# Ranking on TensorE by a triangle matrix, shared angles, and denominators by accumulating DMAs in a fused routing-attention and gated-convolution kernel

## The chip, the cores and the metric

The kernel runs on one core of one Trainium2 chip. The metric is the device time of one execution in microseconds (us). TensorE is called PE here (PEld are its weight loads), VectorE DVE, ScalarE ACT, GpSimd POOL, SyncE SP. A queue name such as SPq is the instruction stream in which an engine issues DMAs.

## The reference

Two parts in a row, all in f32, with batch B = 4, 8 heads, sequence S = 768, head size 64, 16 clusters.

```python
q_assign = argmax(q_n @ c_n, axis=-1)          # nearest of 16 centroids, per head
k_assign = argmax(k_n @ c_n, axis=-1)
mask = q_assign[..., :, None] == k_assign[..., None, :]
scores = where(mask, q @ k.T / 8, -1e9)
attn = exp(scores - max); attn = attn / (sum(attn) + 1e-9)
x = (attn @ v) as [B, S, 512]
x1, x2, x3 = split(x @ w_proj, 3)
x2_conv = irfft(rfft(x2, axis=seq) * rfft(filter, axis=seq))
out = (x1 * x2_conv * x3) @ w_out
```

`argmax` takes the first of equal largest values. Inputs are q, k, v (4, 8, 768, 64), centroids (8, 16, 64), w_proj (512, 1536), filter (768, 512), w_out (512, 512); the output is (4, 768, 512).

## The kernel before

The program is a plan: `build` makes a list of some 1,900 operations, each with the engines that may do it, and `ORDER`, a string written out in the source, gives the order in which they are emitted, the engine of each and the PSUM banks of each matmul group. A word such as `P275:31` is operation 275 on PE, into banks 3 and 1; the letters are P (PE), A (ACT), V (DVE), G (POOL), S (SP). Within one engine the order of the words is the order of its queue. The costs and due times in the source were used to make the string; at run time only the string and the data dependences count.

**Routing and attention.** The 32 heads are taken as 8 groups `n` of four heads, each in two pairs `pr`. `routing(n)` transposes q and k of a group on PE, copies them to `qkP`, casts them to bf16 into `aug`, and makes the masks: products with the normed centroids (`sim`, L582) on PE, two transposes to tokens on DVE (L587), the largest value (L595), equality with it (L596), then for the first of equal values a product with falling weights (L598), another maximum (L601), a difference (L602), the transpose back (L605), and a clip of the k half (L607). DMAs (`masks`, L482) put the 16 rows into `aug`, so that the score matmul adds 0 where the clusters agree and a large negative number elsewhere. Group 0 has its own form of this (`first_masks`).

`attention(n, pr)` has six steps over blocks of 128 keys. A step is three score groups on PE (`sc`), three exponentials of 128x512 on ACT (`exp`, L646 and L649), and eight matmuls with v in f32 (`pv`, L660). The exponentials are also summed over the blocks into `acc` on DVE (L681), the first two blocks by three smaller additions on DVE or POOL (L677). The sum over the 128 partitions gives the softmax denominators. It is done in two ways, chosen by `FIRST`: for groups below `FIRST` and for the last group by matmuls with ones (`den`, L694); for the others by three accumulating DMAs issued by POOL (64, 32 and 16 rows added, L714), a way through memory (L718, L720), a reduce on DVE (L724) and an added constant (L725). Both go on with a reciprocal (L727), a way through memory (`dr`, `rb`) and the division that writes `xT` (L760).

**Convolution.** `hyena(b)` follows each two groups: token products (`U`, L797), spectra (`spectrum`), products with the filter's spectrum (L821, L825), the inverse (`I`), gates (`G`), and the output products (`W`), copied to `ob` and stored. It fills PE between the steps of later groups. For the last batch row block 5 is copied as a whole and stored by one DMA (L919, L922).

**Start.** `angles` makes the sine tables `fw` from index products reduced to one turn, all on DVE, from half-integer indices `s0t` which `half` (L964 to L967) makes on DVE; `tables` transposes them and transforms the filter.

Of the kernel before, what the change touches and what calls it, by code (L numbers as in the profile page):

```python
# [34 lines left out]
FIRST = 2  # L35
# [89 lines left out]
V0 G30 A35 S45 A46 P14:0 G18 S47 P2:1 A48 P9:2 G27 V22 S49 P6:3 P10:4 G24 S52 P1:5 V59 P4:6 G23 V36 V37 S51 P12:7 V38  # L125
V60 A39 G25 P13:0 V53 A50 G17 V61 P8:1 A40 G20 V54 P16:2 V62 G34 P11:3 V55 P5:4 G19 P15:5 P3:6 V21 V56 A63 P68:7 V41
P70:0 A66 G29 A58 P76:1 S121 A64 P74:2 A57 P7:3 V26 G65 P42:4 G32 S123 V71 A67 P146:5 V69 G28 P138:6 S124 P140:3 V44
P149:0 V43 G152 P142:7 A77 V141 S122 P94:4 V75 A147 P96:3 A148 V95 A79 P144:1 P102:2 S126 V72 P100:5 A145 V78 P80:4
S125 A101 V103 A97 P82:1 S127 V81 A98 G105 P108:5 S128 V83 A151 G73 A139 P106:3 A104 V84 S120 V85 G132 P251:2 A99 S242
V86 S134 V107 A150 P245:4 G133 V87 P249:1 S135 A246 P243:6 V88 A252 S130 G33 V89 A250 G31 A244 S131 P257:0 G137 V90  # L130
A248 P255:3 V91 S286 V92 P183:2 V93 A258 V109 P185:1 S129 G247 A256 P187:6 V143 P190:0 A184 V110 S288 P261:4 G136 V111
P263:5 A262 P192:3 V112 P194:7 A264 V113 P200:2 G358 A186 P267:45 V114 A191 V115 A188 G197 A193 P202:1 V268 P204:0
P208:6 A203 V269 P210:3 G198 A195 P212:1 V270 P189:45 A201 A211 V199 A205 P216:7 V117 P196 V271 A116 A209 V119 V207
P218:2 A217 P220:3 P224:0 A213 P226:6 P206 A118 V153 A225 V155 P228:7 A221 P293:1 P214 V157 A219 V272 A229 V160 A227
P295:0 P222 A294 V154 A296 V158 P297:3 V215 P230 A298 A259 P300:2 V273 P302:7 A232 G156 P304:6 P310:1 P312:0 A303
P299:45 A301 V274 A305 V161 P314:3 A311 P306 V162 A254 V275 G159 A266 P318:7 P320:2 P322:6 S280 A313 V223 P164:1 A315
S278 P163:0 A165 S292 P316 A167 V276 A319 V231 S277 P172:3 A321 P178:7 S283 A323 P171:2 S279 A169 P326:6 V166 G308
P324 S287 A327 V168 A175 S285 V170 G309 P328:0 A173 P233:6 S284 V176 A329 S290 P330:1 V174 G253 A234 P177:0 A331
P334:3 S291 V179 P336:6 G307 A181 P338:2 P359:1 V180 S235 P332 A339 V182 S282 A337 G260 A265 S281 P361:0 P419:267 V317
A335 A362 A360 P363:3 P340 S454 V421 A420 A422 V325 S236 A364 P366:0 S289 P368:1 A342 P370:2 P376:6 S453 P378:7 A371  # L140
V333 P380:3 P365:45 A367 S418 A381 A369 P384:2 V237 P386:0 V341 A377 P388:3 S238 P392:1 A385 P372 A387 A379 V373
P394:6 A389 P343:2 V375 V374 P427:073 A344 V383 A393 S239 A395 S240 P396:2 P400:1 A430 S352 P402:6 P382 A401 V391 S345
A403 S458 A428 P390 A397 S456 A429 V399 A424 P404:1 P461:6 P435:20 A431 V241 A405 S346 A423 P463:3 G434 V437 S455
P465:7 P468:1 A462 V436 P398 A466 G353 S457 G354 V407 A464 A469 P470:6 P472:0 P478:2 A425 P406 V438 G426 A473 G356
V439 P480:7 P482:3 A408 P486:1 P409:0 V440 A471 V441 A487 P467:45 G476 A410 V347 A479 S348 A481 G355 V475 P488:6 S411
P490:1 P494:0 A489 V442 P496:2 P498:7 A483 P502:6 V443 G477 P474 A499 A495 S446 A497 V444 P484 V485 A491 S445 A503
S448 P504:3 P701:702 S412 V493 S447 S460 P506:1 P492 A507 S452 V501 A702 S350 A703 P500 S349 A505 S520 V509 P639:6
S459 P641:1 P643:3 A640 P508 A642 V413 A704 G432 S414 A644 P646:6 P648:1 S449 G357 V433 P511:0 A649 A510 V654 P650:2
P656:7 P658:3 A512 V351 P660:1 A647 P645:45 S513 A657 G653 S735 A659 P664:0 A651 S450 P666:6 P668:7 A661 P672:3 V655
S451 P652 A667 S415 V663 A673 S514 A669 P674:2 P709:163 S416 A665 A675 S737 V671 P676:7 S736 P662 A712 A677 V710 A711  # L150
P680:0 V515 P682:2 V679 S516 P684:7 P743:1 A683 P745:3 P670 A685 A681 V417 A713 P717:62 V687 A744 S517 A708 S518
P747:7 P750:0 P752:1 V719 G689 P678 A751 V718 A746 G706 V720 A714 P686 A748 V721 P754:0 P760:2 V722 A688 P762:6 P764:3
V723 P768:7 A753 P749:45 A763 V519 A755 P770:1 A761 V758 P772:6 P521:0 A769 G690 V724 A765 P776:2 V759 A771 P778:7
P523:3 A779 V725 G705 A522 P531:1 A777 S734 V524 P533:7 A773 V726 V757 S733 P780:0 P784:2 G691 V525 P756 A781 S727
V767 S728 S730 P766 S729 V775 S742 P526:6 S738 P786:3 P528:0 A527 V707 S740 A785 V783 P774 A532 S739 S700 P788:6
P805:2 V534 S732 G715 P807:1 A789 P782 V529 A787 S692 A806 S741 V530 G537 P809:6 P812:3 V535 P814:2 P790 A813 V536
A815 V539 A808 P867:073 V791 A810 A792 S693 P816:2 P540:1 A870 V538 S731 G793 P543:6 A869 P811:45 V541 S804 A817 A868
V544 V542 P822:2 G546 P548:0 A823 V545 P824:3 P826:7 P830:1 P556:2 V547 A831 P551:6 V549 A874 G820 P818 V552 A827 V550
A825 G554 P559:1 P832:7 V553 P834:3 P564:0 A833 V555 G794 A835 P838:6 P566:7 V557 A565 G819 P568:3 V558 V567 P840:0
P828 A569 G821 V694 A872 V560 A841 P875:273 G716 V561 A839 V695 A871 G795 V829 S696 P842:0 S903 P846:1 A876 P836 A878  # L160
S904 V563 A877 A847 V837 P848:6 P883:23 A849 S698 A843 A881 G562 S796 P850:7 V884 P909:1 P911:6 S907 V885 P844 A912
V845 S697 A851 A910 S901 P572:02 P913:3 S797 P916:6 A573 V886 G873 P918:7 P920:1 A917 S866 P852 V574 A919 S902 V887
A914 P926:6 P928:7 V575 P570:3 A927 V888 A854 P930:0 V853 P579:2 A921 P581:6 A931 P915:45 A580 V699 A879 A882 V889
P583:1 G576 A929 P934:0 V571 P585:2 G890 A584 V798 A935 P587:73 V586 P936:1 V799 P938:0 P922 A937 S800 V577 G855 A939
V891 A588 G925 P942:2 P932 V590 S894 V589 S896 V892 V578 P944:1 S893 P594:0 S801 V923 P596:3 S895 V582 P946:7 P940
V924 S906 A947 A945 V933 S905 A943 G856 P950:6 P952:7 A595 P954:1 S802 P598:2 A951 S908 V597 A880 P948 V941 S898 A953
S970 A955 P1089:0 P1091:6 P1093:3 A1090 P1096:7 P1098:1 V949 A1092 P1100:0 P956 A1094 A1101 A599 G857 P1106:6 V957
A1097 P600:3 A1099 P1151:027 A1107 A958 V592 G959 P1108:1 P1110:6 A1152 V1153 P1095:45 A1109 V601 A1154 V803 A1111
P1114:1 P1116:3 V591 P1159:027 S858 A1117 G593 S900 A1115 S897 P602:63 A1160 V1161 S1191 P1118:1 V1162 P1102 A603
A1119 S899 G960 V605 S859 V604 P1167:02 V1103 S1185 V1105 S1192 G607 P1122:7 V1169 S1187 P1124:1 P609:3 V1168 A1125  # L170
G606 S1188 P1126:6 A1156 V1170 P1130:0 P1132:2 P611:1 S1189 G961 A1131 V1171 A1123 P1112 S1186 A1158 V1172 V608 A610
P1134:0 P1193:7 A1127 P1120 V1173 A1165 G1104 A1135 V860 P613:3 V1113 P615:6 A614 S962 A1163 P1195:0 P1197:3 P1128
A1196 V861 G1155 V612 S862 A1133 V616 A1194 P1200:0 P1202:1 V1121 A1198 P1136 A1201 A1203 P1204:2 V1174 S963 P617:67
A1138 S863 V1129 P1210:3 A1205 P1212:0 P1214:1 S864 A618 P1199:45 A1213 S1190 A1211 V1208 A1215 P1218:2 S1150 P1220:0
V1207 P1222:3 P1226:1 A1221 P1206 V1137 A1223 A1219 P1228:0 P1230:3 V1175 P1234:2 G1209 P1216 A1231 A1235 V964 A1229
G1139 V965 P1236:3 V619 P1238:2 S966 P1224 A1237 V620 A1157 V622 V621 A1239 P1317:036 V865 A1227 V1217 P1325:721 S967
A1320 S968 A1166 S1254 P1232 A1164 V623 A1319 G1140 V1225 A1326 P1240 A1318 A1327 P624:0 V1176 A1242 V969 S1179 P626:3
A625 S1180 V1233 A1328 S1177 P981:6 S1178 P971:0 A982 S1182 G1141 V1241 P973:1 A972 A627 P629:2 V974 G1243 P983:7 V975
P976:6 V984 V1322 P978:0 S1142 A977 V985 S1358 P1255:3 P1257:1 V979 P1259:6 A1256 P631:7 S628 A1260 V980 G986 A1258
P1262:3 P1264:6 P1266:0 P1272:1 A1265 V987 P1261:45 S1143 G1244 A1273 V989 S1355 A1263 V988 A630 P990:6 S1353 P993:1  # L180
A632 V991 P1014:3 S1316 A1267 V992 P1016:2 S1181 G1271 A1015 V994 S1183 P998:7 V995 P1274:0 S633 P1276:6 P1280:3 A1275
V996 P1018:1 S1351 G997 V999 P1001:0 A1019 P1268 A1281 V1002 A1277 V1000 G1004 P1282:1 V1003 P1006:3 A1283 P1284:6
# [46 lines left out]
def build(T):  # L229
# [385 lines left out]
    def attention(n, pr, sins):  # L615
# [88 lines left out]
        if not last:  # L704
# [5 lines left out]
            else:  # L710
# [12 lines left out]
                def gather(e):  # L723
                    T.nc.vector.tensor_reduce(T.dn, T.dp[:].rearrange("p r b -> p b r"), axis=AX, op=Alu.add)  # L724
                    T.nc.vector.tensor_scalar(T.dn, T.dn, EPS * S, None, op0=Alu.add)  # L725
# [467 lines left out]
```

## Time and profile before

| | |
|---|---|
| median of 3 runs | 368.99 us (368.93 to 369.77) |
| the profiled execution | 369.5 us, span of the trace 367.7 us |
| PE, DVE, ACT, POOL busy | 354.2, 345.0, 269.3, 131.9 us |
| mean granted PE clock | 0.994 |
| DMA moved | 45.69 MB, mean 124 GB/s |

The span runs from the first to the last instruction of the trace. Busy time is the union of an engine's instructions; the share of busy time is an average over stages with different limits, so the stages are looked at one by one. In the strips of the page the span has 40 slices, 9.2 us each, and a digit is a busy share in tenths.

### The profile page before, as it was taken

The page shows a single profiled execution, that of the slowest core. Times are in us where ns is not written, and L with a number is a line of the kernel's source. Part 1 is how long each engine was busy: PE and PEld are TensorE (multiplying, and loading weights), DVE is VectorE, ACT ScalarE, POOL GpSimd, SP SyncE. Part 2 cuts the span into 40 slices and gives each one's busy share as a digit, 9 for nine tenths or more (in the row PEclk, how much of TensorE's full clock was granted, in tenths as well). Part 3 has the DMA queues.
Part 4 walks back from the last instruction along what each step waited for, and adds up shares of the span by engine and source line. Part 5 has one row for each costly group of instructions (what it writes and reads, how often), then busy time and mean ns, then how long its engine had stood idle before and what let it go on. Part 6 is the DMA issues. An engine that isn't in the chain of part 4 may idle for free.

```text
span 367.7 us, 8518 instructions
## 1 busy us (share of the span) xinstructions
PE 354.2 (96%) x3269; PEld 211.6 (58%) x3269; DVE 345.0 (94%) x476; ACT 269.3 (73%) x501; POOL 131.9 (36%) x162
## 2 busy tenths in 40 slices
PE   7879999999999999999999999999989999999994
PEld 3535555455455556655565666665646666567782
DVE  8999999996999999988999999999989999999993
ACT  5979999979785789596986777989858665533251
POOL 7770250533032552425231542413330543135600
PEclk9989999999999999999999999999999999999999
DMA  9994156579555767599775957666553554110124
GB/s 171 235 252 94 29 119 184 101 124 214 122 74 121 161 104 146 99 178 154 101 180 104 210 142 174 111 116 109 92 78 70 146 102 112 47 44 2 59 116 172
DMA packets 88004, 45.69 MB, mean 124 GB/s; under 512 B 76488, under 2 KB 82012, under 8 KB 87964
## 3 DMA queue, kind: packets, MB, share of 16 engines
q1 hardware_dynamic: 82508, 34.77, 40.9%
q0 software_dynamic: 2960, 9.77, 17.7%
q10 hardware_dynamic: 2496, 0.62, 0.9%
q8 instruction: 25, 0.41, 0.5%
q14 instruction: 15, 0.12, 0.1%
HBM read 31.59 MB, written 7.40 MB: 106 GB/s over the span
## 4 chain that ended last, share of the span: by engine, by line
PE 60%; DVE 22%; DMA 6%; issue 5%; ACT 3%; SPq 1%; POOL 1%; DVEq 0%; POOLq 0%; ACTq 0%
PE bank L69 30%; PE pair L660 19%; DVE acc L681 7%; PE bank L797 3%; DMA rb<-dr 3%; DMA aug<-ohT 2%; PE bank L582 2%; PE bank L551 2%; PE bank L67 2%; ACT tm L442 1%; ACT p L649 1%; DVE tm L809 1%; DMA dr<-dn 1%; DVE acc L677 1%; DVE hm L446 1%
## 5 line engine op out<-in xcount | busy, mean ns | idle before, releaser
L660 PE MATMUL pair<-p,vraw 128*64 128x385 f32 x768 | 140.4, 488 | 0.0
L649 ACT ACTIVATE p<-bank 128x512 f32<-128x512 f32 x192 | 109.0, 607 | 22.9 <-PE bank L69 18.5
L681 DVE TENSOR_TENSOR acc<-p,acc 128x1536 f32<-128x1536 f32 x64 | 113.0, 1766 | 2.9 <-POOL acc L677 1.2
L660 PEld LDWEIGHTS pair<-p,vraw 128*64 128x64 f32 x768 | 56.4, 136 | 47.4 <-issue 40.1
L69 PE MATMUL bank<-aug,aug 80*64 80x256 bf16 (+3 forms) x706 | 79.2, 326 | 2.6 <-DMA aug<-ohT 1.5
L646 ACT ACTIVATE p<-bank 128x512 f32<-128x512 f32 x96 | 57.4, 607 | 14.6 <-PE bank L69 13.6
L69 PEld LDWEIGHTS <-aug 80*64 80x64 bf16 (+1 forms) x706 | 43.4, 109 | 41.0 <-issue 28.9
L69 PE MATMUL bank<-xT,wpj 128*64 128x384 bf16 x504 | 50.0, 326 | 0.0
L714 POOL DMA_DIRECT2D acc<-acc x30 | 23.9, 796 | 58.8 <-DMA acc<-acc 29.1
L69 PEld LDWEIGHTS <-wpj 128*64 128x64 bf16 x504 | 33.4, 110 | 11.0 <-issue 3.7
L677 POOL TENSOR_TENSOR acc<-p,p 128x512 f32<-128x512 f32 x21 | 27.0, 1297 | 32.2 <-DVE acc L677 11.5
L246 ACT CAST aug<-qkP 64x768 bf16<-64x768 f32 x43 | 35.4, 829 | 0.7
L69 PEld LDWEIGHTS <-y 128*64 128x64 bf16 x496 | 28.2, 110 | 10.2 <-issue 3.0
L246 ACT COPY qkP<-bank 128x512 f32<-128x512 f32 (+1 forms) x50 | 25.7, 551 | 9.4 <-PE bank L69 7.0
L248 POOL CAST aug<-qkP 64x768 bf16<-64x768 f32 x16 | 14.1, 884 | 42.5 <-DVE xT L760 17.9
L821 DVE TENSOR_TENSOR tm<-bank,hm 128x512 f32<-128x512 f32 x44 | 27.9, 683 | 0.8 <-POOL y L825 0.2
L69 PE MATMUL bank<-wout,y 128*64 128x512 bf16 x192 | 24.5, 379 | 0.1
L825 POOL TENSOR_TENSOR y<-tm 128x512 bf16<-128x512 f32 x14 | 17.8, 1276 | 14.6 <-DVE tm L821 10.0
L797 PE MATMUL bank<-wpj,xT 128*64 128x512 bf16 x192 | 22.8, 380 | 0.0
L899 POOL TENSOR_TENSOR y<-yy,x 128x768 bf16<-128x768 f32 x6 | 11.0, 1825 | 26.9 <-DVE yy L896 19.4
L677 DVE TENSOR_TENSOR acc<-p,p 128x512 f32<-128x512 f32 x27 | 18.3, 701 | 0.4 <-ACT p L646 0.3
L246 ACT COPY ob<-bank 128x512 f32<-128x512 f32 x20 | 11.4, 592 | 9.8 <-PE bank L69 9.8
(163 smaller groups left out, 457.6 us busy)
## 6 DMA issues: line engine op xcount, KB each, us to landing
vraw<-in_v_dram SPq DMA_DIRECT2D x16, 384.0 KB, 5.7
qkraw<-in_k_dram SPq DMA_DIRECT2D x31, 192.0 KB, 4.9
qkraw<-in_q_dram SPq DMA_DIRECT2D x30, 192.0 KB, 4.2
rb<-dr SPq DMA_DIRECT2D x30, 192.0 KB, 3.7
out_dram<-ob SPq DMA_DIRECT2D x11, 512.0 KB, 4.7
acc<-acc POOLq DMA_DIRECT2D x10, 384.0 KB, 5.0
acc<-acc POOLq DMA_DIRECT2D x10, 192.0 KB, 4.2
wpj<-in_moe_w_proj_dram POOLq DMA_DIRECT2D x4, 384.0 KB, 6.2
```

Source lines behind the costliest of these rows:

```text
L69: T.nc.tensor.matmul(out[64 * i:64 * i + 64], lhsT[:, 64 * i:64 * i + 64], rhs, start=start, stop=stop)
L246: T.nc.scalar.copy(out, in_)
L248: (T.nc.vector if e == "DVE" else T.nc.gpsimd).tensor_copy(out, in_)
L646: T.nc.scalar.activation(o, ap(h).rearrange("p (a b) -> p a b", a=2), Act.Exp, scale=0.125)
L649: T.nc.scalar.activation(flat(s)[:, lo:lo + 512], ap(h), Act.Exp, scale=0.125)
L660: T.nc.tensor.matmul(o[64 * hp:64 * hp + 64, ch, :385], T.vraw[vs][:, hp, sk * D:(sk + 1) * D], T.p[slots[sk]][:, hp, 384 * ch:384 * ch + ...
L677: alu(e).tensor_tensor(o, x, y, op=Alu.add)
L681: T.nc.vector.tensor_tensor(T.acc[os], T.p[slots[sk]][:, :, :S], T.acc[os], op=Alu.add)
L714: op(("POOL", .8), lambda e, rows=rows: T.nc.gpsimd.dma_start(flat_()[:rows], flat_()[rows:2 * rows], accum_op=Alu.add), te, r=[], w=AK, b ...
L797: T.nc.tensor.matmul(ap(h)[64 * i:64 * i + 64], T.xT[xs][:, kt, tokens(m, i, w_)], T.wpj[:, kt, DM:2 * DM], start=kt == 0, stop=kt == ND - 1)
L821: op(("DVE", .68), lambda e, i=i, cs=cs, r=r, h=h: T.nc.vector.tensor_tensor(T.tm[r][:, cs], ap(h), hmrow(i, (0, 2, 2, 3)[2 * r + cs]), op ...
L825: op({"POOL": 1.3, "DVE": .68}, lambda e, i=i, r=r: alu(e).tensor_tensor(T.y[:, i, r], T.tm[r][:, 0], T.tm[r][:, 1], op=Alu.add if r else ...
```

## The change

Four edits, and a new `ORDER` for all operations with 1,963 words instead of 1,936.

1. Groups 1 to 7: L598, L601, L602 and L607 are gone. The equality words are transposed, multiplied on PE by a 128x128 matrix `tri` (blocks of 16: 1 on the diagonal, -2 for earlier clusters; the k half times 262144) into two banks, and four clips of 64x384 on ACT or DVE bring them back to `ohT`. POOL makes `tri` at the start. The masks wait for the clips of both chunks.
2. The angles: POOL makes odd integers directly, `half` is gone, `s1t` is one POOL instruction; some angle instructions may be on ACT (Copy, Abs) or POOL, and for the second table one DVE instruction becomes a product (DVE) and a sum (POOL).
3. `FIRST` from 2 to 1: the two pairs of group 1 get their denominators by accumulating DMAs. In that way the constant is added on ACT instead of DVE (L725).
4. The last output row is copied in halves on ACT and DVE, and stored by two DMAs, issued on ACT and SP.

```diff
-FIRST = 2
+FIRST = 1
...
-                op(("POOL", 1.1), lambda e, w_=w_, m=m: T.nc.gpsimd.indirect_dma_start(
+                op(("POOL", 1.7), lambda e, w_=w_, m=m: T.nc.gpsimd.indirect_dma_start(
...
-        op({"DVE": .58, "POOL": 1.8}, lambda e: alu(e).tensor_tensor(
-            words(), words(), T.revx[:].unsqueeze(1).to_broadcast([128, 48, NC]), op=Alu.mult), b0 + 4, r=["revx"],
-           w=both("oh"), lock=True)
-        op(("DVE", .95), lambda e: V().tensor_reduce(m2(), words(), axis=AX, op=Alu.max), b0 + 4.1, r=both("oh"), w=both("m2"))
-        op({"DVE": .75, "POOL": 1.8}, lambda e: alu(e).tensor_tensor(words(), words(), bc(m2()), op=Alu.subtract),
-           b0 + 4.2, r=both("m2"), w=both("oh"), lock=True)
...
-        op(("DVE", .38), lambda e: V().tensor_scalar(T.ohT[64:], T.ohT[64:], -1.0, 1.0, op0=Alu.max, op1=Alu.add), due,
-           r=both("ohT"), w=both("ohk"), lock=True)
+        h2 = Bank(cls, 2)
+
+        def rank(e, h=h2):
+            for ch in range(2):
+                columns(bank(h.ids[ch])[:, :384], T.tri[:], T.ohT[:, ts(ch, 384)], True, True)
+        op(("PE", .325), rank, due, r=both("ohT") + both("ohk") + ["tri"], w=[h2], alloc=h2, kind="proj")
+        for ch in range(2):
+            for j in (1, 0):
+                def clip(e, ch=ch, j=j, h=h2):
+                    o, x = T.ohT[64 * j:64 * j + 64, ts(ch, 384)], bank(h.ids[ch])[64 * j:64 * j + 64, :384]
+                    if e == "DVE":
+                        V().tensor_scalar(o, x, 0.0 if j else -1.0, None, op0=Alu.max if j else Alu.add)
+                    elif j:
+                        T.nc.scalar.activation(o, x, Act.Relu)
+                    else:
+                        T.nc.scalar.activation(o, x, Act.Copy, bias=-1.0)
+                op({"ACT": .48, "DVE": .55}, clip, due + .6 + .1 * ch, r=[h2], w=[("ohk" if j else "ohT", ch)], free=[h2])
...
-                    T.nc.vector.tensor_scalar(T.dn, T.dn, EPS * S, None, op0=Alu.add)
-                op(("DVE", .68), gather, te + 6, r=["dp"], w=["dn"], kind="port")
+                op(("DVE", .48), gather, te + 6, r=["dp"], w=["dn"], kind="port")
+                op(("ACT", .22), lambda e: T.nc.scalar.activation(T.dn, T.dn, Act.Copy, bias=EPS * S), te + 6.1, r=[], w=["dn"])
...
+                if last and tt == 2 and e_:
+                    for c, e in ((0, "ACT"), (1, "DVE")):
+                        op((e, .37), lambda e, c=c, ob=ob, h=h: copy(e, ob()[:, 1, ts(c, 256)], ap(h)[:, ts(c, 256)]), due + 1,
+                           r=[h], w=[(obk[1], c)], free=[h], after=[])
+                        op({"SP": .6, "ACT": .6}, lambda e, c=c, ob=ob: dma(e)(
+                            T.out[b].rearrange("(p t) m -> p t m", t=NT)[:, 5, ts(c, 256)], ob()[:, 1, ts(c, 256)]), due + 2,
+                           r=[(obk[1], c)], byts=131e3)
+                    continue
...
-        def half(e):
-            for i in range(2):
-                h = T.s0t[64 * i:64 * i + 64]
-                T.nc.vector.tensor_scalar(h[:, :2 - i], h[:, :2 - i], 0.5 - 383.0 * i, None, op0=Alu.add)
-            h = T.s0t[64:, 1:]
-            T.nc.vector.tensor_scalar(h, h, -1.0, 767.5, op0=Alu.mult, op1=Alu.add)
-            T.nc.vector.tensor_scalar(T.s1t, T.s0t, 1.0 / S, None, op0=Alu.mult)
-        op(("DVE", 1.0), half, .3, r=["s0t0"], w=["s0t", "s1t"])
+        op({"DVE": .3, "POOL": .3}, lambda e: alu(e).tensor_scalar(T.s1t, T.s0t, 0.5 / S, None, op0=Alu.mult), .3,
+           r=["s0t"], w=["s1t"])
...
+        def tri(e):
+            G().memset(T.tri, 0.0)
+            sel = lambda op_, fill, pattern: G().affine_select(out=T.tri, in_=T.tri, compare_op=op_, fill=fill, base=0,
+                                                               pattern=pattern, channel_multiplier=1)
+            sel(Alu.is_ge, -2.0, [[-1, 128]])
+            sel(Alu.not_equal, 1.0, [[-1, 128]])
+            sel(Alu.is_ge, 0.0, [[-16, 8], [0, 16]])
+            G().tensor_scalar(T.tri[:, 64:], T.tri[:, 64:], BIG, None, op0=Alu.mult)
+        op(("POOL", 1.5), tri, 10, w=["tri"])
```

In the new `ORDER` the operations that the prediction names stand as follows ("..." for words left out). Group 2's transposition is V446 and its ranking P447, P481 is a `pv`; groups 3, 5 and 7 have V733 and P734, V1189 and P1190, V1645 and P1646. G518 is the first accumulating DMA of group 1's second pair, P531 the first `U`. At the end P1958 finishes the last row's matmuls, V1961 and A1959 copy its halves, and A1951 and S1952 are the copy and the store of rows 2 and 3.

```diff
... V446 P481 A504 G413 V484 A498 P447:13 A502 V350 G431 P505:7 S351 P509:0 A448 V450 P511:2 A449 P491 ...
... V1189 P1234 A1183 G1226 A1247 P1254:6 A1253 P1190:72 P1242 ...
... P1953:1 P1958 P1954 P1940 V1961 P1942:5 V1955 S1962 A1941 P1943 S1956 P1947
P1949:3 A1944 V1948 P1950 S1945 A1951 A1959 S1952 A1960
```

The costs of some operations in the source are also set anew (for example the indirect DMA above); they have no effect at run time.

More of the change, by code (lines that the diff above doesn't have):

```diff
@@ L130 @@
[L130 to L134, printed above, removed]
@@ L150 @@
[L150 to L154, printed above, removed]
```

260 lines of the change are left out of this document (145 added, 115 removed).

## The prediction

> **What bounds the kernel now.** I read the page first, then the busy time by stage, the chain, the waits, the groups kept apart by shape, and the start and the end instruction by instruction. Part 1 of the page and the strips of part 2:
>
> ```profile
> span 367.7 us, 8518 instructions
> ...
> PE 354.2 (96%) x3269; PEld 211.6 (58%) x3269; DVE 345.0 (94%) x476; ACT 269.3 (73%) x501; POOL 131.9 (36%) x162
> ...
> PE   7879999999999999999999999999989999999994
> ...
> DVE  8999999996999999988999999999989999999993
> ...
> PEclk9989999999999999999999999999999999999999
> ```
>
> Two engines are nearly full, so the question is which one sets the end. The table by stage (columns: stretch, its length, busy time and count of PE, PEld, DVE, ACT, POOL, then clock, DMA share, GB/s) answers it:
>
> ```profile
> 0.00:9.00 9.00, 6.53 (x29) 3.26 (x29) 7.43 (x25) 4.99 (x10) 6.81 (x30) 1.00 0.94 170
> 9.00:20.00 11.00, 8.11 (x79) 4.77 (x79) 10.55 (x24) 10.78 (x23) 8.25 (x23) 1.00 1.17 244
> 20.00:35.00 15.00, 14.59 (x105) 7.71 (x107) 14.27 (x25) 12.49 (x25) 5.71 (x6) 0.89 0.83 178
> ...
> 50.00:75.00 25.00, 25.00 (x209) 12.87 (x208) 24.37 (x25) 24.18 (x46) 8.01 (x9) 1.00 0.60 137
> ...
> 355.00:368.00 13.00, 8.03 (x83) 5.42 (x79) 6.49 (x10) 2.73 (x6) 0.00 (x0) 0.95 0.33 129
> ```
>
> PE is idle for 367.7 - 354.2 = 13.5 us in all: 2.47 + 2.89 + 0.41 = 5.8 before 35 us, 12.7 - 8.03 = 4.7 after 355, and so only 3.0 in the 320 us between. DVE work taken out there can win back at most about those 3.0 us; PE work put in there costs its full length. The start is the other way round: DVE and ACT are full while PE waits. The first score matmul and the first exponential:
>
> ```profile
> 20.11 0.50 PE L67 MATMUL bank<-aug,aug 80*128 80x512 bf16 x2 [2.07 <-DVE aug L526]
> ...
> 20.54 0.60 ACT L649 ACTIVATE p<-bank 128x512 f32<-128x512 f32 x1 [0.18 <-PE bank L67]
> ```
>
> The chain gives PE 60% and DVE 22%; it runs along DVE from 52 to 125 us, where PE is busy beside it, so DVE is the next limit there.
>
> **DVE, by rows.** What the change removes, with the rows of the groups by shape (busy, mean ns):
>
> ```profile
> L601 DVE TENSOR_REDUCE m<-oh 128x48 bf16<-128x768 bf16 x7 | 6.6, 949 | 0.1
> ...
> L602 DVE TENSOR_TENSOR oh<-oh,m 128x768 bf16<-128x768 bf16 x5 | 5.3, 1066 | 0.1
> ...
> L598 DVE TENSOR_TENSOR oh<-oh,revx 128x768 bf16<-128x768 bf16 x7 | 4.4, 627 | 0.2
> ...
> L725 DVE TENSOR_SCALAR dn<-dn 128x12 f32<-128x12 f32 x10 | 3.4, 340 | 0.3
> ...
> L607 DVE TENSOR_SCALAR ohT<-ohT 64x768 bf16<-64x768 bf16 x7 | 2.7, 382 | 0.2
> ```
>
> That is 22.4 us. The half-integer set-up (L964 to L967) was 1.8 and four angle instructions (one L346, one L350, two L353) 2.1: 26.3 in all. Added: 8 of the 28 clips (the others are ACT's in the new order), 64x384 from a bank, by the 128x384 copies of a bank on DVE at 0.548: 4.4; two more gathers of 0.48; one angle product of 0.43: 5.8. The new order also hands work about: counted by the letters of the same operations, DVE takes 10 more casts of q and k (0.535), 5 more folds (0.575), 3 output copies (0.688) and 2 copies of transposes (0.687), and gives 5 products y (0.687), one of y2 (0.95) and 2 small copies, about +8. Net 345.0 - 26.3 + 5.8 + 8 = 332.5.
>
> **ACT and POOL.** ACT gets 20 clips at 0.482 (the row of its 128x384 copies), 12 additions to the sums at 0.2 (its 128x1 rows), three angle instructions at 0.48, loses 15 casts at 0.829, two denominators at 0.5 and a few copies: 269 to about 267. A rule speaks against these clips: the Trainium skill, "ScalarE: Activation LUTs", Rules for kernel authors, says to do relu and add on VectorE, up to about 3x faster per element in bf16. Here the source is an f32 bank and the rows are 0.482 on ACT against 0.548 on DVE; by the rule 20 clips would win some 6 us of ACT time if moved, by the rows nothing. No Relu or Abs is in this trace; copies beside exponentials and sines cause no table load there (three loads, of 1.28 each, one each at L306, L307 and L370), so I take none for the new ones; a load before and after each of the 9 Relus is the upper bound, 23 us of ACT time. The same page (Table sets) puts relu, copy and abs into every table set, which no run here shows yet.
>
> POOL gets 6 accumulating DMAs at 0.80, the five instructions of the triangle (about 1.8, by its 0.41 select and scale rows), and net 5 casts and 5 products: 132 to about 141.
>
> **PE.** Seven rankings of four half-array matmuls of 384 columns: the row of that shape (504 in 50.0 us) gives 0.40 each, 2.8. The two denominators of group 1 leave (48 of L694 in 5.1, 8 each): 1.7. Net **+1.1** in a stretch where PE has no room. As low as 0.2 if a ranking takes the 0.27 of one 384-column pair hidden by overlap, as high as 1.8.
>
> **The start.** Of the DVE instructions ahead of the last mask of pair 0 (put, 20.83 us), 1.8 of set-up, 2.1 of angles, 0.43 of centroid copies, 1.1 of two casts, 0.55 of a copy and 0.57 of the second pair's transpose are gone or behind it, 6.5; a product and two table copies come in, 0.9; and DVE waits about 1.3 longer at first, since POOL now does a 0.47 iota pair and three extra iotas ahead of the angle inputs. The last mask comes some 4 us earlier, near 17. ACT doesn't follow: walking its new order with the same rows, the first exponential stands behind about 19 us of its own work, near 19.8 (-0.7). After it, ACT sat idle 0.82 and 1.32 before 26.3 us, waiting for PE; with scores already made those 2.1 us can go too. Bounds 0 to -2.8, I take **-1.7**, near the middle, since PE's transposes still share banks with the scores.
>
> **The middle.** Two effects. DVE has 12 us less to do over the run, and the masks of a group (transposition, clip, then a DMA) come 0.63 + 0.95 + 1.07 earlier on DVE, less the ranking and two handovers. The 3.0 us of PE idle there is the ceiling: half, **-1.5**. Against it PE now waits itself for DVE's transposition, in seven places, and scores queue behind it. In the new order of groups 2, 3, 5 and 7 only one attention step (1.30 by the chain, or 1.5 with a score) stands between V446, V733, V1189, V1645 and their rankings, and the transposition takes 0.97: 0.33 to spare. Before, PE hardly ever waited on masks:
>
> ```profile
> PE bank L69 <- DMA aug<-ohT: 1.5, 2, 0.9
> ```
>
> Bounds 0 to +5.8 (below); I take **+0.5**, DVE on time in most. The addition to dn on ACT puts two handovers into a chain that SP waits for; it is covered: for group 1's second pair the rows give 5.0 + 4.2 + 3.8 + 2.9 + 3.4 for its DMAs, 0.9 on DVE and ACT, twice 3.7 for dr and rb, 1.0 for xT, 28.6 us, and between G518 and the first token product P531 PE has 16 steps of 1.30, 52 scores of about 0.22 and 7 us of routing work, 39. Without that cover the loss would be the whole excess. SP swaps four DMAs of 6 KB for four of 96 KB there, off the path.
>
> **The end.** The last matmul ends near 363.0, ACT's copy (0.59) and the 512 KB DMA issued at 363.68 end the span at 367.7. In the new order row 5 is done ahead of it in halves, but A1951 and its DMA S1952 still come last with the same size, and A1959 only follows that copy. So only 131 KB issued 0.4 later competes with it: bounds -0.4 to +0.4, I take **-0.2** since less is in flight. That the halves shorten the end is thus not so.
>
> **Sum.** -1.7 + 1.1 - 1.5 + 0.5 - 0.2 = -1.8. The profiled execution took 369.5 with a span of 367.7; the median of the runs is 368.99. New span 365.9, forecast 368.99 - 1.8 = **367.2 us**. A difference under 0.3% (1.1 us) can't be told from none.
>
> **Rivals.** *A, slower: PE stands at the rankings.* If DVE has one accumulation (1.77) too many ahead, a tight ranking comes 1.77 - 0.33 = 1.4 late, and PE loses that each time: four groups, +5.8, 373.0; in two of them, +2.9, 370.1. It decides from a lag of 0.33 us. For it: DVE is still over 90% busy and its accumulations are its longest instructions; the token products start nine steps later (after 40 instead of 31), in a stretch where ACT is at 24.18 of 25. Against: POOL and ACT now carry more. Chance 0.24.
> *B, the start doesn't move.* ACT, with tables and copies, already sat at 10.78 of 11 us, and the weights' DMA for wout now precedes the filter loads where the DMA share is over 1. Then 367.2 + 1.7 = 368.9. Chance 0.16.
> *C, the clock stays up.* The granted clock was 0.5 for 3.4 us from 21.8, after PE had been nearly idle from 17.6 to 20.1 (the third digit of PEclk); that cost up to 1.7 us of PE. With scores from 17 us the gap closes and more of the middle's idle goes: 367.2 - 1.7 - 1.0 = 364.5. Chance 0.14. The Trainium skill, "TensorE: Matmul & The Clock Gate", What's actually happening, says that an idle window of about 3.4 us halves the clock and that the windows run free, so the gap need not even close, only shrink; the trace agrees with the length.
> The forecast itself has 0.46, between 365.5 and 368.5.
>
> **How the numbers follow.** Faster by over 0.3% (under 367.9): C's 0.14 and 0.38 of the forecast, 0.52. Same: 0.08 of the forecast and 0.13 of B, 0.21. Slower (over 370.1): A's 0.24 and 0.03 of B with a late load, 0.27. The range leaves out the worst of A and the best of C: 364.2 to 371.2.
>
> **What would show it.** DVE near 332 busy and no L598 to L607 clip; the first exponential before 20.2 us; no third dip in PEclk for C; PE idle ahead of the ranking lines under 0.5 in all, against 3 to 6 for A; a span's end still 4.6 us behind the last matmul. I am wrong if the middle loses PE time to a wait that before didn't have, most likely on DVE's transposition or on masks.

## The result, and the profile after

The changed kernel takes 374.6 us (median of four runs, 374.14 to 375.39) against 369.38 for the kernel before in the same measurement: 1.0143 times as long, 95% interval 1.0119 to 1.0167. Forecast was 367.2, range 364.2 to 371.2. The profiled execution after took 374.14 with a span of 372.4, that of before 369.5 with 367.7, so there are 4.7 us to be found.

The page after, parts 1 and 2:

```profile
span 372.4 us, 8625 instructions
...
PE 356.2 (96%) x3289; PEld 211.2 (57%) x3289; DVE 335.2 (90%) x459; ACT 267.5 (72%) x515; POOL 146.0 (39%) x178
...
PEclk9999899999999999999999999999999999999999
```

DVE (forecast 332.5) and ACT (267) came out about as reckoned and POOL 5 over its 141, yet the time rose. The dip in PEclk has moved from the third digit to the fifth. The table by stage (columns as in the prediction) shows the place, first the kernel before, then the changed one:

```profile
0.00:35.00 35.00, 29.23 (x212) 15.74 (x214) 32.25 (x71) 28.26 (x56) 20.77 (x58) 0.95 0.97 197
35.00:50.00 15.00, 14.69 (x118) 7.63 (x116) 14.71 (x17) 14.06 (x26) 6.32 (x6) 1.00 0.23 55
```

```profile
0.00:35.00 35.00, 30.86 (x228) 17.24 (x230) 29.52 (x60) 30.30 (x61) 28.69 (x66) 1.00 1.00 201
35.00:50.00 15.00, 12.16 (x85) 5.96 (x83) 12.71 (x18) 10.02 (x20) 5.87 (x8) 0.89 0.50 107
```

So the start won 1.6 us of PE's idle time, as forecast, and the half clock besides, and in the next 15 us PE stood 2.8 us and ran the rest at 0.89. PE's waits (us in total, times, longest) name who it waited for, against the 1.5 on masks that stood there before:

```profile
PE bank L69 <- POOL tri L1015: 2.7, 1, 2.7
...
PE bank L69 <- DMA aug<-ohT: 0.9, 1, 0.9
```

And the chain in that window, in order of time (start, us, what), shows where the triangle came from:

```profile
33.25 1.59 POOL y L407
...
35.14 0.91 POOL tri L1015
...
36.10 2.77 POOL tri L1015
...
39.37 0.41 POOL tri L1020
...
39.81 0.51 PE bank L69 x3
40.33 2.40 PE pair L693 x8
```

GpSimd's four indirect DMAs (L407; L383 in the kernel before), at 15.4 to 22.9 us before, stand at 27.2 to 34.8 in the new order and `tri` behind them. Its three selects then took 0.91, 2.77 and 0.35 us, 4.1 from the first to the last, where the prediction had 0.41 for each. The second, the longest, lay beside three VectorE instructions that followed each other without a gap:

```profile
35.80 0.64 DVE L249 CAST aug<-qkP 64x768 bf16<-64x768 f32 x1
36.37 1.74 DVE L714 TENSOR_TENSOR acc<-p,acc 128x1536 f32<-128x1536 f32 x1
38.03 0.67 DVE L710 TENSOR_TENSOR acc<-p,p 128x512 f32<-128x512 f32 x1
```

The first ranking, P275, was at the head of PE's queue from 36.6; it could begin when the selects ended, and the scaled half of the triangle (L1020) came at 39.8:

```profile
39.33 1.00 PE L69 MATMUL bank<-ohT,tri 128*64 128x384 bf16 x4 [2.71 <-POOL tri L1015]
```

The weighted sum behind it (L693) took 2.4 us for what takes 1.3 at full clock: the granted clock was half from 40.4 to 43.8, as this slice of the table shows.

```profile
41.00:42.00 1.00, 1.00 (x6) 0.39 (x2) 0.97 (x3) 0.98 (x3) 0.54 (x1) 0.50 0.52 43
```

The Trainium skill, "TensorE: Matmul & The Clock Gate", What's actually happening, says that the clock is at half after an idle window of about 3.4 us, and full again after a busy one of that length. The 3.4 at half clock agree with the second; the idle time ahead of them was shorter than such a window, 2.7 us.

### The profile page after: what moved, and what is told of

The parts are those of the page before. It is cut to its first block, busy times and chain, and to the rows that moved or that the text cites. A ratio compares the mean times of both kernels' runs of the same rounds, so it can differ in the third digit from the quotient of the medians.

```text
span 372.4 us, 8625 instructions
## 1 busy us (share of the span) xinstructions
PE 356.2 (96%) x3289; PEld 211.2 (57%) x3289; DVE 335.2 (90%) x459; ACT 267.5 (72%) x515; POOL 146.0 (39%) x178
## 4 chain that ended last, share of the span: by engine, by line
PE 47%; DMA 15%; DVE 14%; issue 8%; POOL 6%; ACT 5%; SPq 2%; POOLq 0%; ACTq 0%; DVEq 0%
PE bank L69 21%; PE pair L693 17%; DMA acc<-acc 8%; DVE acc L714 5%; DMA rb<-dr 3%; PE bank L830 3%; PE bank L575 2%; DMA dd<-acc 2%; POOL y L407 2%; DVE tm L842 2%; ACT p L682 1%; DVE tm L854 1%; PE bank L606 1%; POOL tri L1015 1%; POOL y L858 1%
## 5 line engine op out<-in xcount | busy, mean ns | idle before, releaser
L693 PE MATMUL pair<-p,vraw 128*64 128x385 f32 x768 | 141.8, 490 | 0.2 <-issue 0.2
L682 ACT ACTIVATE p<-bank 128x512 f32<-128x512 f32 x192 | 108.6, 606 | 25.7 <-PE bank L69 20.2
L714 DVE TENSOR_TENSOR acc<-p,acc 128x1536 f32<-128x1536 f32 x64 | 111.9, 1749 | 2.5 <-ACT p L682 0.2
L69 PE MATMUL bank<-aug,aug 80*64 80x512 bf16 (+3 forms) x730 | 83.0, 327 | 2.2 <-DMA aug<-ohT 0.9
L693 PEld LDWEIGHTS pair<-p,vraw 128*64 128x64 f32 x768 | 57.6, 137 | 43.4 <-issue 36.5
L747 POOL DMA_DIRECT2D acc<-acc x36 | 28.8, 800 | 102.1 <-DMA acc<-acc 53.7
L69 PE MATMUL bank<-xT,wpj 128*64 128x384 bf16 x472 | 46.7, 326 | 0.9 <-DVE xT L793 0.7
L69 PEld LDWEIGHTS <-wpj 128*64 128x64 bf16 x472 | 30.1, 110 | 11.5 <-issue 3.7
L69 PEld LDWEIGHTS <-y 128*64 128x64 bf16 x512 | 26.5, 110 | 11.5 <-issue 2.7
L858 POOL TENSOR_TENSOR y<-tm 128x512 bf16<-128x512 f32 x19 | 24.0, 1274 | 13.5 <-DVE tm L854 10.5
L249 POOL CAST aug<-qkP 64x768 bf16<-64x768 f32 x21 | 17.5, 845 | 27.5 <-DVE dn L760 12.8
L247 ACT CAST aug<-qkP 64x768 bf16<-64x768 f32 x28 | 23.0, 829 | 0.7 <-PE bank L69 0.3
L932 POOL TENSOR_TENSOR y<-yy,x 128x768 bf16<-128x768 f32 x7 | 12.8, 1822 | 13.9 <-DVE dn L778 7.2
L575 PEld LDWEIGHTS bank<-ident,qkraw 128*128 128x128 f32 x144 | 15.6, 141 | 4.5 <-ACT p L682 1.4
```

The source lines that it names most:

```text
L69: T.nc.tensor.matmul(out[64 * i:64 * i + 64], lhsT[:, 64 * i:64 * i + 64], rhs, start=start, stop=stop)
L247: T.nc.scalar.copy(out, in_)
L575: T.nc.tensor.transpose(bank(h.ids[i // 4])[:, block(i % 4, 2 < i < NT)], raw(ss[i // NT], i % NT), T.ident)
L682: T.nc.scalar.activation(flat(s)[:, lo:lo + 512], ap(h), Act.Exp, scale=0.125)
L693: T.nc.tensor.matmul(o[64 * hp:64 * hp + 64, ch, :385], T.vraw[vs][:, hp, sk * D:(sk + 1) * D], T.p[slots[sk]][:, hp, 384 * ch:384 * ch + ...
L714: T.nc.vector.tensor_tensor(T.acc[os], T.p[slots[sk]][:, :, :S], T.acc[os], op=Alu.add)
```

## The experiments

Ratios are to the kernel before on the same chip, with 95% intervals. Runs of one kernel spread over some 5 us there, so small differences are told by the interval alone. In the diffs, words of `ORDER`.

### The triangle

**e1: the triangle early.** `tri` (G24) goes right behind G34, ahead of the indirect DMAs; nothing else.

```diff
- ... A306 A297 G24 V225 A301 ...
+ ... A190 G34 G24 V116 S289 ...
```

> The changed kernel with one word moved: POOL makes the triangle (G24) right behind the small constants (G34, near 23 us) instead of behind the four indirect DMAs (near 35 us). Theory 1 (the loss is PE standing at the first ranking until POOL has made the triangle: 2.71 us idle there, and the half clock for 3.41 us that follows, up to 1.7 us): 374.6 - 4.4 = 370.2 us, PE idle ahead of the first ranking under 0.3, no dip of the clock near 40 us. Rival (the loss sits in the many small waits of a fuller middle, and time won early is given back there): 373.0 us or more, with the PE idle after 50 us grown by 3.

369.72 us, ratio 0.9997 (0.9954 to 1.004): the whole loss is gone. The selects' group and the first ranking in e1's profile:

```profile
L1015 POOL TENSOR_SCALAR_AFFINE_SELECT tri<-tri 128x128 bf16<-128x128 bf16 x3 | 0.9, 309 | 0.2
```

```profile
36.44 0.53 PE L69 MATMUL bank<-ohT,tri 128*64 128x384 bf16 x4
```

No wait ahead of it, no half clock while PE works, selects at 0.31. This run shows the cause of the loss against the kernel before. It doesn't bring the forecast's gain: that was a ratio of 0.995, below the interval. The next three take the loss apart.

**e10: what slows a select.** 24 selects of the same shape on an unused tile, in e1.

```diff
+            G().affine_select(out=T.spare, in_=T.spare, compare_op=Alu.is_ge, fill=-2.0, base=0, pattern=[[-1, 128]],
```

> The kernel of e1 with 24 further selects of the triangle's shape on an unused tile, in eight groups of three on GpSimd between 36 and 75 us, where no indirect DMA is near: the output doesn't use them. Theory (a select is slowed fourfold where VectorE adds up exponentials in f32 at the same time): those beside a running accumulation of line 714 take 1.0 us or more each, the others 0.3 us. Rival (the four indirect DMAs just ahead of the triangle slowed it): all 24 take 0.3 us. The time may rise by up to 1 us.

380.3 in the one run. Two of GpSimd's eight groups of three and one of its own additions (start, us), and what VectorE did beside them:

```profile
58.34 1.01 POOL L1025 TENSOR_SCALAR_AFFINE_SELECT spare<-spare 128x128 bf16<-128x128 bf16 x3
59.31 1.79 POOL L711 TENSOR_TENSOR acc<-p,p 128x512 f32<-128x512 f32 x1
...
64.11 4.33 POOL L1025 TENSOR_SCALAR_AFFINE_SELECT spare<-spare 128x128 bf16<-128x128 bf16 x3
```

```profile
58.62 0.75 DVE L471 SCALAR_TENSOR_TENSOR hm<-bank,hw,tm 128x512 bf16<-128x512 f32 x1 [0.76 <-ACT tm L467]
...
59.89 2.83 DVE L715 TENSOR_TENSOR acc<-p,acc 128x1536 f32<-128x1536 f32 x1
...
64.67 7.78 DVE L715 TENSOR_TENSOR acc<-p,acc 128x1536 f32<-128x1536 f32 x4
```

One by one in the trace, the selects at 58.34 took 0.29 each, beside an operation that reads a bank; of those at 64.11 the first took 0.67 and the two that began during an accumulation of two tiles (L715 here, L714 in the changed kernel) 1.73 and 1.79, as long as the accumulation, with no indirect DMA near: the theory holds. It can cost either side. The accumulations beside those two selects took their usual 1.76, but the one at 59.89, begun while GpSimd added two tiles itself, took 2.83. The Trainium skill, "SBUF — State Buffer", SBUF: two separate sides, says that a VectorE operation with two SBUF inputs and a GpSimd operation that reads SBUF lock each other out for whole instructions; the rows agree. The 10 us that the run lost are more than the expected 1. In its trace PE waits 2.5 us for a cast on GpSimd (L250), and the clock falls to 0.93 in 50 to 75 and in 100 to 125 us; the rest isn't taken apart.

**e11: the ranking later instead.** In the changed kernel, P275 goes behind P302 and P235, and its clips behind it.

```diff
- ... P321:2 P275:31 A322 P302:45 A277 V310 A316 A279 P235:2 V276 A278 V156 G356 A318 ...
+ ... P321:2 A322 P302:45 V310 A316 P235:2 P275:31 V156 V276 G356 A318 A277 A279 A278 ...
```

> The changed kernel itself with the triangle left where it is, behind the four indirect DMAs on GpSimd, and the first group's ranking matmuls moved two steps later in TensorE's order, behind the second half of one weighted sum and the row sums; the three clips and a cast that follow them go behind one more piece of work on their engines. Theory (the late triangle costs only because the ranking stands first in TensorE's queue then): the wait of 2.7 us falls under 0.7, the half clock after it disappears, ratio to before 1.000 to 1.003. Rival (the wait is taken over by who needs the ranked words, the masks of the second group): the waits of TensorE in 35 to 60 us stay over 3 us, ratio over 1.008.

375.65 us, ratio 1.0131 (1.0073 to 1.0188): the median won nothing, and the rival's wait is there. PE's waits from 30 to 60 us:

```profile
PE bank L69 <- ACT ohT L638: 1.7, 1, 1.7
PE bank L69 <- POOL tri L1015: 0.8, 1, 0.8
```

1.7 + 0.8 is nearly the old 2.7. The triangle gates the ranking and its clips, and the next scores (P325) take a bank of the ranking, which is free only when a clip on ScalarE (L638) has read it. This profiled run took 371.54, without a half clock, and another 371.88 at a mean clock of 0.998; the other four took 375.6 or more at 0.992 to 0.994. So where the clock stayed up part of the loss was won back, as the theory had it, but in most runs it didn't.

**e13: the wait filled.** Matmuls whose products nobody reads, ahead of P275 (16 as built, of the whole array, not 32 halves).

```diff
+            op(("PE", 2.6), warm, due, r=both("ohT") + both("ohk") + ["identb"], w=[h3], alloc=h3, free=[h3])
```

> The changed kernel itself, triangle late as it is, with 32 matmuls of the ranking's shape on words that are already there put into TensorE's order just ahead of the first ranking: they fill the wait and their products are read by nobody. Theory (of the 4.9 us lost, 2.7 are the wait and about 2 the half clock that follows 3.4 us later): no half clock at 40 to 44 us, the time falls by 1.7 to 2.2 us, ratio to before 1.008 to 1.010 against 1.0143. Rival (what follows the wait is set by VectorE and ScalarE, and TensorE's clock there is hidden): ratio stays at 1.013 or more.

374.33 us, ratio 1.0107 (1.0058 to 1.0157), profiled at 373.6. In its profile the clock is full and the wait down to 0.5:

```profile
36.64 2.77 PE L67 MATMUL bank<-ohT,identb 128*128 128x384 bf16 x16
39.91 0.50 PE L67 MATMUL bank<-ohT,tri 128*128 128x384 bf16 x2 [0.49 <-POOL tri L1027]
```

1.0107 against 1.0143 is 1.3 us, near the 1.7 that 3.4 us at half clock are worth, but the intervals overlap: the division of the loss, some 3 us of wait (2.7 by the trace) and under 2 of clock, stays an estimate.

### The end of the kernel

**e2** is e1 with A1959 and A1960, the second copy and store of the last row's halves, right behind V1961. **e6** is e1 with the two 512 KB rows finished and stored first and the halves last:

```diff
- ... P1958 P1954 P1940 V1961 P1942:5 V1955 S1962 ... S1945 A1951 A1959 S1952 A1960
+ ... A1941 P1943 V1944 S1945 P1947 A1948 P1950 V1951 S1952 ... A1955 S1956 P1957:3 P1958 A1959 V1961 A1960 S1962
```

> As e1_tri_early, and the copy of the last row's first half and its store (A1959, A1960) placed right behind the other half's copy instead of behind the last copy of all. Theory (the span ended 5.9 us after the last matmul group began, against 5.1 before, because a second copy of 0.38 and a store on ACT come after the last large copy): 0.8 less than e1_tri_early, 369.4 us, the end 5.1 us behind the start of the last group. Rival (the 512 KB store of the last rows sets the end in both): no difference, 370.2.

> The kernel of e1 with another order at the very end: the two output rows of 512 KB are computed, copied and stored first, and the last row's two halves of 256 KB come last. Theory (the two 512 KB stores, issued 1.1 us apart in the changed kernel, set its end): the stretch from the last matmul's start to the end of the span falls from 5.8 us to about 4.6, and the time by about 1.0, to a ratio of about 0.997. Rival (the same bytes must leave in the same last microseconds whatever their order): the stretch stays within 0.3 us of 5.8 and the time as e1, ratio 1.000.

1.0019 (0.9981 to 1.0057) and 1.0002 (0.9966 to 1.0037); from the last matmul's start to the end of the span 5.64 and 5.85 us, against 5.89 in the changed kernel, 5.84 in e1 and 5.07 before. Neither order of the stores brought the 0.8 back: the 0.2 of e2 is no more than e11, whose end is the changed kernel's, differs from it (5.61). What sets the end isn't settled by these two.

### Where the start's gain went

In e1 PE idles 4.1 us in the first 35 (before: 5.8) and loses no clock there (before: 1.7), so by these two traces it is 3.3 ahead. Against e15 and e16 (below), which start like before (first score at 20.11 and 20.12) but idle 4.6 and 4.7 there, it is 2.2 to 2.3. The table by stage and PE's waits (in brackets) in e1:

```profile
100.00:125.00 25.00, 22.69 (x186) 11.99 (x181) 20.81 (x27) 16.87 (x32) 6.11 (x8) 1.00 0.83 158
```

```profile
111.89 0.52 PE L69 MATMUL bank<-aug,aug 80*64 80x512 bf16 x4 [0.46 <-DMA aug<-ohT]
112.84 1.17 PE L69 MATMUL bank<-aug,aug 128*64 128x256 bf16 x12 [0.43 <-DMA aug<-ohT]
...
118.61 1.52 PE L693 MATMUL pair<-p,vraw 128*64 128x385 f32 x8 [0.88 <-DMA vraw<-in_v_dram]
```

2.3 us of idle time, where before had 0.3; 1.8 of it is by name on group 3's masks and v. These stand in SP's queue behind the row-sum broadcast.

**e3** takes the accumulating DMAs out of e1 (`FIRST = 2`; group 1's sums by PE again).

> As e1_tri_early, with FIRST back at 2: group 1's denominators by matmuls with ones and two small DMAs, placed seven PE operations behind the pair's last accumulation; everything else in its order. Theory (the accumulating DMAs of group 1 hold SP and POOL and with them the masks of group 3, 1.1 us of PE idle at 115.8 us; against it PE does 1.7 us more): about the same as e1_tri_early, 370.2 to 370.8. Rival a (the accumulating DMAs are free and the matmuls cost their full length and a bank): 371.9. Rival b (they hold up more than the one wait): 368.5.

372.72 us, 1.0126 (1.0077 to 1.0175). The wait on the masks stayed, 1.7 us in one piece, so the accumulating DMAs are not its cause. In this order they are worth 3.0 us by the medians and 4.8 by the ratios, more than any of the three expectations said; rival a came nearest.

**e5** puts v (S711) and the first pair's masks ahead of the broadcast (S421), and the second pair's behind. **e9** adds e6's end.

```diff
- ... S522 ... S739 A791 P778 V770 S421 ... S746 ... S743 ... S740 ... S742 S741 ... S744 ... S711 ... S745 ...
+ ... S522 ... S711 S739 A791 P778 V770 ... S740 P889:263 S742 S741 S421 S746 S743 S744 S745 ...
```

> The kernel of e1 (changed kernel, triangle built early on GpSimd), with one change in the order of the sync engine's queue for group 3: the load of v and the masks of the first pair are issued ahead of the row-sum broadcast that waits for the exponentials' sums, the masks of the second pair behind it. Theory (what the start gained is given back at 110 to 125 us, where TensorE waits 2.3 us for masks and v that stood in that queue behind the broadcast): the idle time of TensorE in 100 to 125 us falls from 2.3 us to under 0.8, the time to about 367.7, a ratio to before of about 0.995. Rival (the next limit, DMA share of 0.9 in that stretch or VectorE, takes its place): the idle time moves to 125 to 175 us and the time stays at about 369.7, ratio 1.000.

> The edits of e5 and e6 together on the kernel of e1. If both theories hold, -2.0 and -1.0 us from 369.7, about 367.0 and a ratio of 0.992 to 0.993; if the rivals hold, 369.7 and 1.000.

e5 1.0 (0.9968 to 1.0032), e9 0.9982 (0.9954 to 1.0011). The idle time didn't leave: 2.3 us in 100 to 125 and 1.4 in 125 to 150 (0.3 in e1), now under other names. PE's waits in e5, 100 to 150 us:

```profile
PE bank L575 <- ACT p L682: 1.0, 1, 1.0
PE bank L830 <- DVE xT L793: 0.7, 1, 0.7
PE bank L69 <- DVE qkP L249: 0.7, 1, 0.7
```

**e7** gives e1 the angles and the half's set-up of before, on VectorE.

> The kernel of e1 with the angles and the half's set-up computed as in the kernel before, all on VectorE; ranking on TensorE, accumulating DMAs and the halves of the last row stay. Theory (what the start gains is given back later at the queues, so taking it away costs nothing): the first score matmul starts again at about 20.1 us, against 19.1, and the time stays within 0.5 us of e1, ratio 1.000. Rival (the start's gain reaches the end): the time rises by 1.5 to 2.5 us, ratio about 1.005.

0.9997 (0.9968 to 1.0026), in the same session as e5 and e6, which have the early start, at 1.0 and 1.0002. That is the theory's number, but its condition wasn't met: the first score matmul came at 19.41, not 20.1 (e1: 19.08), and there was no half clock at the start. So the run gives back a third of a microsecond, less than its interval can show, and whether the start's gain reaches the end isn't shown by it. It shows something else: with the angles back on VectorE two thirds of the earlier start stay, so most of it comes from the rest of the change and its order, and not from the shared angles.

### Parts of the change alone

**e4** is the kernel before with the ranking alone, in the order of before. **e8** is e1 without it (L598, L601, L602, L607 of before back on VectorE), **e12** is e8 with `FIRST = 2`.

> The kernel before with the ranking by the triangle alone, in the order of before: in each group one to five PE operations behind the transposition, clips half on ACT and half on DVE, the triangle made near 18 us. Theory (PE sets the end, so the ranking costs its 2.8 us, and DVE's 12 us saved win back only part of 3.0 us of PE idle): 369.4 + 1.3 = 370.7, between 369.7 and 372.2. Rival (DVE, which carries the chain from 52 to 125 us, is the real bound there): 367.0 or less.

> The kernel of e1 (changed kernel, triangle early) without the ranking on TensorE: the scaled maximum and the subtraction go back to VectorE as in the kernel before; shared angles, accumulating DMAs and the halves stay. Theory (with the triangle out of the way TensorE sets the time, so the ranking's matmuls cost what they take): the time falls by 2.3 us from 369.7 to about 367.4, ratio 0.994. Rival (VectorE is as close to the bound, and gets 9 to 10 us of work back): the time rises to 371 or more, ratio 1.004.

> The kernel of e8 with FIRST = 2, so without accumulating DMAs too: of the change, the shared angles and the halves are left. With e1, e3 and e8 it makes a square of two by two. Theory (the DMAs are worth some 3 us and the ranking costs some 2 to 3, the two cancel): the time is that of the kernel before, 369 to 370, ratio 1.000, and e8 lies 3 us below it. Rival (the two parts belong together, since the ranking's relief of VectorE is what lets the rest move up): this one is over e3's 1.013, at 1.015 or more.

382.14 us, 1.0388 (1.0306 to 1.047); 385.04, 1.0402 (1.0357 to 1.0448); 385.02, 1.0413 (1.0368 to 1.0458). e4 missed both of its numbers, and e8 and e12 lie on their rivals' side, but far beyond their figures. The likely reason, not shown, is that an order written for one set of operations doesn't carry another: e8's VectorE is busy 351.5 us, 16 more than e1's, and the time rises by 15. The sums by DMA, worth 3.0 with the ranking, are worth nothing without it. So the parts can't be priced one by one in these orders. But 4.3 of the 13 us that e4 lost show rival A as it was described, PE standing for VectorE's transposition:

```profile
PE bank L69 <- DVE ohT L612: 4.3, 4, 1.5
```

### VectorE's relief by itself

**e15** (before) and **e14** (e1) have the accumulations narrowed, **e18** is e9 with the same. They leave 76 of the 768 columns out of the row sums, so they price VectorE's work and are no versions to use:

```diff
-                    T.nc.vector.tensor_tensor(T.acc[os], T.p[slots[sk]][:, :, :S], T.acc[os], op=Alu.add)
+                    a_ = T.acc[os][:, :, :692]
+                    T.nc.vector.tensor_tensor(a_, T.p[slots[sk]][:, :, :692], a_, op=Alu.add)
```

> The kernel before with the same narrower accumulations, 692 of 768 columns, so with about as much relief of VectorE as the change gives (11 us against 10), and nothing else of the change. The forecast's step (middle, relief of VectorE worth 1.5 us): the time falls by 1.5 us, ratio 0.996. Rival (TensorE's own chain of matmuls sets the middle and the relief is worth nothing): ratio 1.000.

> The kernel of e1 with VectorE's 64 accumulations of exponentials over 692 of the 768 columns of each half, so that VectorE does some 11 us less; the left-out columns fall out of the row sums. Theory (with the triangle out of the way TensorE sets the time and VectorE's relief buys only the waits that name it, 4 us in e1): the time falls by 1 to 2 us, ratio 0.995 to 0.997. Rival (VectorE is as much the bound as TensorE): by 4 us or more, ratio 0.989 or less. Third (the waits only change their names): ratio 1.000.

> The kernel of e9 (triangle early, masks and v of group 3 ahead of the broadcast, new order at the end) with the narrower accumulations of e14, 692 of 768 columns, so VectorE has 11 us less; the left-out columns fall out of the row sums. Theory (in the changed kernel the sync engine's queue and VectorE limit the stretch of 100 to 140 us in turn, so relieving either alone gave nothing: e5 1.000, e14 0.998): both together give 2.5 us or more, ratio 0.993 or less. Rival (neither holds it; TensorE's own work does): ratio as e14, 0.997 to 0.999.

e15: 0.9895 (0.9849 to 0.9942), so 3.9 us for 9.5 of VectorE's work (344.96 to 335.46 busy). e14: 0.9978 (0.9946 to 1.001), 0.8 us for 9 (335.12 to 325.91). e18: 0.9952 (0.9917 to 0.9986), about what e9 and e14 give together. By these runs VectorE's relief is worth more in before's order than PE's 3.0 us of idle time in the middle allowed, and in the changed kernel little of that is left. The trace of e15 doesn't show where: it is of a run at 368.18, 2 us over their median, and in it PE's idle time from 35 to 360 us falls from 3.1 to 1.8, near the forecast's 1.5. Whether SP's queue and VectorE limit the stretch in turn isn't settled: e18 lies between its two theories.

**e16** and **e17** try to get the relief with all work done: six of the 128x512 sums on GpSimd, in before and in e9.

```diff
- ... A211 V199 A205 ... A379 V373 ...
+ ... A211 G199 A205 ... A379 G373 ...
```

> The kernel before with six of the first sums of two exponential tiles (128x512) moved from VectorE to GpSimd, at places where GpSimd is idle for 2 us or more: 4 us less on VectorE, 8 us more on GpSimd. A try for a faster version: e15 priced VectorE's relief in this order at 3.9 us for 11, so 1.4 us, ratio 0.996. Rival (the sum takes 1.3 us on GpSimd against 0.7, and the accumulation behind it waits for it): ratio 1.000 or more.

> The kernel of e9 with six such sums moved from VectorE to GpSimd in the same way. By e14's price (0.8 us for 11) 0.3 us, ratio 0.998 like e9; if the relief acts as in e15, 1.4 us, ratio 0.994. Rival (the accumulations behind the slower sums wait): ratio 1.002 or more.

1.0024 (0.9997 to 1.0052) and 1.0073 (1.0039 to 1.0107): the rivals' numbers. The traces show two reasons. In e16 VectorE wasn't relieved at all: its busy time is 346.4 us against 345.0, and four of the 21 sums left to it took 1.5 to 1.8 us instead of 0.68. In e17 it fell by 1.7 us, and the accumulations waited 3.5 us for GpSimd's slower sums. No version here that does all the work beats the kernel before by what can be told; e9 comes nearest.

## Why the prediction was wrong, by its own steps

The steps against the profiled runs (us, after or e1 less before; busy and idle by the tables by stage, with a cut at 360 us for the end):

| step | forecast | after | e1 |
|---|---|---|---|
| start: PE's idle time before 35 us | -1.7 | -1.6 | -1.7 |
| PE: busy (half clock: before 1.7, after 1.7, e1 none) | +1.1 | +2.0 | +0.1 |
| middle: PE's idle time, 35 to 360 us | -1.5 + 0.5 | +3.5 | +2.5 |
| end: from 360 us, idle | -0.2 | +0.8 | +0.8 |
| sum | -1.8 | +4.7 | +1.7 |

(e1's profiled run took 371.16, 1.4 over its median, so its middle is somewhat too dark.)

- **POOL, the step that failed.** The triangle was priced "about 1.8, by its 0.41 select and scale rows" into GpSimd's total, as time of an engine with room. When it would be done was never set against P275, and the tight rankings counted were those of groups 2, 3, 5 and 7. It was the first ranking that failed, on GpSimd, with 4.1 us for the selects, behind four DMAs that had moved back 12 us. e1, which moves this one word, takes away the whole loss, some 5 us; it still lies 2.5 over the forecast, for what stands under Middle and End.
- **Start.** The size came out: the first score matmul at 19.06 (20.11 before), the first exponential at 19.47 (20.54), behind ScalarE's work as the prediction had it (PE's 1.5 us of wait there is for a cast on ScalarE). Part of the 1.6 is the run: in e15 and e16, with the same start as before, the half clock began at 20.2 and 20.0 instead of 21.8, and PE idled 1.0 to 1.1 less ahead of 35 us. That the gain reaches the end was taken for granted. e1 is ahead at 35 us and level at the end, but no run here shows the way in which it goes.
- **Clock.** Rival C had the mechanism: the half clock of the start did go (1.7 us), and in the changed kernel it came back 18 us later, behind the wait for the triangle.
- **PE.** The seven rankings measure 3.5 us in e1 (0.50 each, priced 0.40) and the two denominators give 1.7 (48 in 5.1 before, 32 in 3.4): +1.8, the upper bound that was given.
- **Middle.** -1.5 for the relief was under-sized for before's order by e15's runs (3.9, from 2.1 to 5.6), though not by its trace (1.3). +0.5 for new waits was far under-sized: in the changed kernel the triangle alone is 2.7, and even in e1 the waits outweigh the relief by 2.5. Of e1's 5.6 us of idle time there, 2.3 lie at 100 to 125 (1.8 by name) and 1.8 after 300, where the longest wait, 1.4, is for VectorE's L894; what makes these late was only argued. The prediction's own sign of being wrong, a wait in the middle that before didn't have, came, though not on the transposition or the masks that it named.
- **Rival A** came on its side (slower) and near its number (373.0), by PE standing at a ranking, but at one place, for GpSimd, and not for VectorE's lag. That its number is so near is luck.
- **End.** Forecast as no gain; the stretch grew by 0.8. The two 512 KB stores, issued 2.15 us apart before, were issued 1.1 us apart; that this is the reason isn't shown (e6).
- **Tables.** No load came with the nine Relus on ScalarE (L638), as taken, and as the Trainium skill, "ScalarE: Activation LUTs", Table sets, has it. A fourth load did come, for the angle product that is now ScalarE's first instruction.
- **Small sums.** The work that the new order hands about adds up to some 7 us on VectorE by the rows given, not 8. GpSimd's rise to 141 comes out only if the five folds and two differences (L602) that leave it, 8.0 us, are counted too. Neither enters the time.

## What to carry to other kernels

When a change adds a small operand that an engine at its bound will wait for once, follow that operand's first use through every queue that makes it, also on an engine with 60% idle time, and price its instructions beside what the other engines do at that moment. Time won at the start isn't yet time won at the end: here a kernel that was 2 to 3 us ahead at 35 us was level at the end, so before counting such a gain, look for the stretches where a transfer or another engine already meets its need with nothing to spare. In a kernel whose order is written out, a part taken out or put in by itself is measured together with an order that doesn't fit it, so an experiment that moves one word tells more than one that removes a feature.

## What the hardware showed that was not expected

A GpSimd select of 128x128 bf16 took 0.29 to 0.35 us beside a VectorE transposition or an operation that reads a bank, and 1.73 and 1.79 when it began during one of VectorE's f32 additions of two tiles in SBUF (1.76). The other way round, such an addition took 2.83 when it began during GpSimd's own. So work moved from VectorE to GpSimd can come back as time on VectorE (e16). GpSimd's four indirect DMAs took 0.94 to 1.49 us before and 1.06 to 2.39 in the changed kernel, where the two that began during accumulations took 2.39 and 1.59. PE's waits of 2.07 us (before) and 2.71 us (changed kernel) were followed by 3.4 us at half clock. A wait's length alone doesn't decide it: in e7 one of 1.78 was followed by 3.4 us at half clock, in e12 one of 2.66 wasn't.
